# Turning x by VectorE instead of ScalarE, transform results by ScalarE alone, and a new order of all engines, in a spectral and state-space mix

## The chip, the cores and the metric

The kernel runs on one core of one Trainium2 chip. The metric is the device time of one execution in microseconds (us); lower is better. Each engine (TensorE for matmuls, VectorE, ScalarE, GpSimd, and SyncE, which only issues DMAs) works through its own list of instructions in the order in which the program gives them, and waits at an instruction until what it needs is there.

## The reference

One input x of 2048 rows (time) and 1024 columns goes two ways, and a gate per row mixes the results:

```python
x = A_x                                                    # (1, 2048, 1024), bf16
g = _sigmoid((x * gate_w).sum(-1, keepdims=True))
a = irfft2(rfft2(x) * (w_r + 1j * w_i))                    # over both axes
# the state-space way, for each t in turn:
h = Lam_bar[None, :] * h + Bu[:, t, :]                     # Bu = x @ B_bar.T, complex, 1024 states
b = 2.0 * (hseq @ Cmat.T).real + x * Dskip
return g * a + (1 - g) * b
```

## The kernel before

**Turning x.** Both ways need x with its columns on the partitions. The rows are taken in 16 groups: group j holds the 128 rows `16 p + j`. Groups 0 to 11 are loaded as they are into tiles `xn` (L242, called `CT` in the trace, because the space is used again for C later), turned by TensorE into a PSUM tile `pt` (L919, 8 transposes of 128 by 128 per group), and copied from there into the big tile `xQ` by ScalarE (L929). Groups 12 to 15 come turned from a transposing DMA (L238) and are copied into `xQ` by ScalarE from SBUF (L925). In `xQ` time stands as chunk c (8 chunks of 256), half g (2), group j (16), step q (8); the p of a group is thus `(c, q, g)`, and the copy L929 reads `pt` with a step of two elements, so that the halves g come apart. The trace gives every such copy as 128x1024, bf16.

**The spectral way, at the beginning.** `fold()` (L943 to L954, VectorE) makes sums and differences of columns out of `xQ` for each group or pair of groups into `preT`, TensorE multiplies by a cosine table (`fd`, L433 to L443), the result goes to SBUF as `X` (`fd_out`, L449, 16 casts of 128x1024 from PSUM), TensorE does the first stage along time (`s1`, L462), and the result goes to SBUF as `CT`, `A` or `A_last` (`s1_out`, L474, 16 casts of 128x1024 from PSUM). Of these casts VectorE does 4 of L449 (`FD_DVE`) and 3 of L474 (`S1_DVE`), ScalarE the rest. For some groups a mirror matmul (L970) and two sums of VectorE (L976, L977) come between. From there the results go through DRAM to later stages.

**The state-space way.** For each of the 8 chunks `unit_mm` (L398) multiplies all of `xQ` of that chunk with `BT`, in four units of 32 matmuls; it cannot begin before all 16 groups are in `xQ`. ScalarE casts each unit to `h` (L408). VectorE then does the recurrence of the chunk on `h`: products with tables `tab` (L347, L350), sums (L353, L356), two scans (L363), products again, and sums (L374, L378). The tables `tab` are made once at the beginning by `make_tab`, four times over: VectorE makes an angle (L281, L1106, L1108), ScalarE its sine and cosine and their products `t` (L1110, L1111, L1113, L292, L298), VectorE the last two tables (L302, L307). The result `h` is multiplied with C by TensorE (L713, and L727 for the last three tiles of 128 rows). The very last operations are L727 for the last chunk, the closing sum on VectorE (L899), and a store. L892 (VectorE) prepares what L899 adds; L825 to L846 (VectorE) make the output of the spectral way out of its last matmuls.

**The order.** It is written out by hand: the string `ORDER` has one letter for each step of each function above (`T` a transposed group, `U` its copy, `f` a step of `fold`, `F` and `E` `fd` and its cast, `S` and `A` `s1` and its cast, `t` a step of `make_tab`, `h` and `H` a unit of `unit_mm` and its cast, `v` the next step of the recurrence, which `PIECES` then names), and each engine gets its instructions in the order in which the letters stand. `SLOTS` names for each PSUM tile in turn which of four places it takes. SyncE issues nearly all DMAs in that same order. `FILL_V`, `FILL_T` and `WARM` set matmuls without use ahead of the first ones, and are the same in both kernels.

Of the kernel before, what the change touches and what calls it, by code (L numbers as in the profile page):

```python
# [26 lines left out]
NCH = S // TC  # L27
# [5 lines left out]
NTURN = 12  # L33
# [4 lines left out]
FD_DVE = (2, 4, 6, 7)  # L38
# [3 lines left out]
S1_DVE = (1, 4, 5)  # L42
CLOSES = (0, 1, 2, 3, 10, 4, 5, 11, 12, 6, 7, 8, 9)
PIECES = (
# [6 lines left out]
)  # L51
SLOTS = (
    "0123012310231023102310230123012031201312031203101230132031231031201312303312013213021021013010320130",
    "1220123203201320130130120321023120320321021023120312301230231201302303120",
# [3 lines left out]
    "xxxTVUVVVaTfVVrrUGTGG|Tfaaa|UafFffftafftUftxFEfTETUFffU22xSEkSTSTArxAfffUAUFTTEUfffUFbxwxbxbbTUEFbfE",  # L58
    "1bT~SSUfuFSFAUUUU2bbtbfAF1AtbbtrFttrbEffE11EbEh11SStbttfttttAg1~HtfufhA~tetFSSFrKHrtu1EAvfAEhtttvttt",
    "SSFtbbvvvAtEttH1Avthtftv1cttwv1tcthccctttvtcch~HFtvftHvvhuHtvfStEettStAHhtAeKrvFctcvvFhEEHKtvwtcSvtS",  # L60
    "hvvKc1vcc1vAAKKvv1c1v1hcvswcsLMvvveHHekMYsssnNHvvhHnsvvvJWWMvs3vsvNvvsssssnvssnvvs4NMvv4Njvhv553vhvv",
    "YvyJJL46H4vv5WWvhh5vvvMM78Jj7HHmn3nHvv8M44m6MnN77WW5jv+Yy5vvv3M845+mNY8nMJJMyvvv+467hvHMh5vN7N34vHmh",
    "4J8m+6n3h8v77HmH+55v4n64JMvNnMYy5vW83n+v7N474vJ568vYmmNJ7dh7NWj+v58v5vyvvd88MhvHHm8+MJm6h+n378vv7Hh8",
    "J+d4Y4YX5vv5NnJH6XXv7ny7mNNm8+hn8hvqivvvvvJvqyHihYivvyiqhivqqiYvNImvni+qJJmHIIiini+HinvdIIH+vvIIIqIN",
    "IiiiNmI+vvIInvvImvyJqii%NJINIJYJYmhvvv+vvvlylzvhHmplpzZZH+mZZZhlZvhPPRR++zyRRRlQDQHzRZZmRHZ+ZRZvoOZD",
    "QvlpDzzPovOvQBvZZlpPYvZZvBZDZRDRRRvzQDoloOBzoQOopZOoPOBlzlZRoDDZZvBZZRpQvzCvYZZvZZBZZPRDoQoo9RQQ9yRR",
    "0RRyCooD099C9Y990DD0D0Y00",
# [75 lines left out]
def kernel(  # L143
# [82 lines left out]
    x_v = x.rearrange("(p j) d -> p j d", j=16)  # L226
# [7 lines left out]
    def load_x():  # L234
        for i in range(8):
            if i >= NTURN // 2:
                g = i - NTURN // 2
                nc.sync.dma_start_transpose(out=xt[:, :, :, g].rearrange("p j d s -> p (j d) s"), in_=x_sg[g][:, NTURN * D:])  # L238
                yield
                continue  # L240
            for js in (slice(0, 1), slice(1, 2)) if i == 0 else (slice(0, 2),):
                nc.sync.dma_start(out=xn[i][:, js], in_=x_v[:, 2 * i + js.start:2 * i + js.stop, :])  # L242
                yield
# [678 lines left out]
    def turn_out():  # L922
        for j in range(16):
            if j >= NTURN:
                nc.scalar.copy(out=x_gjq[:, :, :, :, j, :].rearrange("p c d g q -> p d g c q"),  # L925
                               in_=xt[:, j - NTURN].rearrange("p d g (c q) -> p d g c q", c=NCH))
                yield
                continue
            nc.scalar.copy(out=x_gjq[:, :, :, :, j, :].rearrange("p c d g q -> p d c g q"),  # L929
                           in_=pts.pop(j).rearrange("p d (c q g) -> p d c g q", c=NCH, g=2))  # L930
# [285 lines left out]
```

## Time and profile before

| | before |
|---|---|
| time, median of 3 runs (lowest to highest) | 305.25 us (305.02 to 307.25) |
| profiled execution: span from first to last instruction | 303.6 us |
| TensorE busy | 296.4 us (98%) |
| VectorE busy | 289.3 us (95%) |
| ScalarE busy | 188.5 us (62%) |
| GpSimd busy | 73.3 us (24%) |
| HBM traffic | 166 GB/s over the span |

The profiled execution is recorded by its span alone, 303.6 us. The median of the runs lies 1.65 us above it, the lowest run 1.42 us; that part stands before the first or after the last instruction, or is the difference between one execution and another. TensorE's granted clock is full throughout (0.999). Busy time of TensorE is modelled on pipelined matmuls and includes short gaps between dependent ones, so its 98% doesn't mean that all of it is work. Durations of neighbouring VectorE instructions overlap a little, so that the sum of single durations is larger than the busy time.

### The profile page before, as it was taken

What the parts mean: (1) busy time and instruction counts of PE and PEld (TensorE: products, weight loads), DVE (VectorE), ACT (ScalarE), POOL (GpSimd) and SP (SyncE); (2) the same over time, 40 slices, a digit from 0 to 9 for tenths busy, and PEclk for the clock granted to TensorE, in tenths of its full rate; (3) what the DMA queues carried; (4) which work ended last, traced back from release to release, by engine and by line L of the source; (5) the groups of instructions that cost most, each with busy time, mean ns of one, the idle gap of its engine ahead of it and who ended that gap; (6) DMA issues with size and microseconds to landing.
All of it is one profiled execution on the core that took longest, in us unless ns stands there. A gap on an engine that the chain in (4) does not pass through costs nothing. (4 is left out here: it accounts for less than half of the span.)

```text
span 303.6 us, 6402 instructions
## 1 busy us (share of the span) xinstructions
PE 296.4 (98%) x2568; PEld 197.4 (65%) x2592; DVE 289.3 (95%) x340; ACT 188.5 (62%) x255; POOL 73.3 (24%) x99
## 2 busy tenths in 40 slices
PE   8999999999999999999999999999999999999995
PEld 5664677878864685458553866669657986645543
DVE  2999999999999999999999999999899999999995
ACT  4999999896532383667665865529668774343400
POOL 2100420745893001110210220202011253252330
PEclk9999999999999999999999999999999999999999
DMA  6999999989999599895948798687758876978976
GB/s 208 341 201 194 253 193 310 162 142 154 268 214 241 160 259 219 181 250 189 212 96 258 163 223 225 139 294 147 242 174 185 165 88 135 160 132 143 165 153 181
DMA packets 74157, 59.35 MB, mean 196 GB/s; under 512 B 44904, under 2 KB 61680, under 8 KB 74128
## 3 DMA queue, kind: packets, MB, share of 16 engines
q1 hardware_dynamic: 66560, 49.82, 65.8%
q0 software_dynamic: 6912, 8.69, 23.0%
q10 hardware_dynamic: 656, 0.44, 0.5%
q8 instruction: 20, 0.33, 0.4%
q14 instruction: 9, 0.07, 0.1%
HBM read 27.46 MB, written 23.08 MB: 166 GB/s over the span
## 5 line engine op out<-in xcount | busy, mean ns | idle before, releaser
L398 PE MATMUL psu<-xQ,BT 128*128 128x256 bf16 x1024 | 116.5, 273 | 0.2 <-DVE X L449 0.2
L398 PEld LDWEIGHTS <-BT 128*128 128x128 bf16 x1024 | 99.0, 98 | 17.3 <-issue 4.6
L713 PE MATMUL ps_y<-CT,h 128*128 128x512 bf16 x397 | 92.5, 379 | 0.9
L363 DVE TENSOR_TENSOR_SCAN h<-rz,h 128x2048 bf16<-128x2048 f32 (+1 forms) x20 | 70.8, 3561 | 0.0
L713 PEld LDWEIGHTS <-h 128*128 128x128 bf16 x416 | 39.6, 98 | 46.3 <-issue 2.9
L785 POOL DMA_DIRECT2D y_scratch<-su x20 | 17.3, 902 | 135.7 <-ACT su L779 105.4
L408 ACT CAST h<-psu 128x1024 bf16<-128x1024 f32 x32 | 32.3, 1011 | 18.7 <-PE psu L398 13.1
L350 DVE TENSOR_TENSOR h<-h,tab 128x4096 bf16<-128x4096 bf16 (+1 forms) x20 | 37.1, 1859 | 0.1
L744 ACT ACTIVATE ye<-ps_y,omg 128x512 f32<-128x512 f32 x26 | 17.9, 689 | 26.3 <-PE ps_y L713 11.8
L347 DVE TENSOR_TENSOR xQ<-h,tab 128x4096 bf16<-128x4096 bf16 x12 | 27.4, 2284 | 1.0 <-ACT h L408 1.0
L603 ACT CAST X<-ps_s 128x1024 bf16<-128x1024 f32 x16 | 16.2, 1010 | 14.6 <-PE ps_s L594 11.2
L727 PE MATMUL ps_q<-CT,h 128*128 128x512 bf16 (+2 forms) x110 | 21.3, 348 | 0.2
L817 ACT ACTIVATE BT<-ps_id,gB 128x1024 bf16<-128x1024 f32 x14 | 15.3, 1114 | 9.9 <-PE ps_id L810 5.7
L671 ACT CAST ZT<-ps_is 128x1024 bf16<-128x1024 f32 x16 | 15.8, 1017 | 6.2 <-PE ps_is L661 6.2
L637 ACT CAST C<-ps_is 128x1024 bf16<-128x1024 f32 x16 | 15.7, 1011 | 5.1 <-DMA xQ<-in_A_x_dram 3.4
L851 POOL DMA_DIRECT2D BT<-y_scratch x10 | 13.1, 1452 | 19.7 <-DVE BT L846 13.3
L727 PEld LDWEIGHTS <-h 128*128 128x128 bf16 x112 | 10.3, 98 | 10.4 <-DVE h L378 0.5
L779 ACT ACTIVATE su<-xs,omg 128x512 f32<-128x512 bf16 x20 | 14.2, 723 | 4.1 <-DMA y_scratch<-su 2.2
L929 ACT COPY xQ<-pt 128x1024 bf16<-128x1024 bf16 x12 | 12.2, 1082 | 1.3 <-PE pt L919 1.3
L449 ACT CAST X<-ps_fd 128x1024 bf16<-128x1024 f32 x12 | 12.3, 1062 | 1.0 <-PE ps_fd L439 0.9
L617 DVE TENSOR_TENSOR UV<-X,Wb 128x2048 bf16<-128x2048 bf16 x8 | 9.6, 1220 | 0.6 <-ACT ye L744 0.6
L617 DVE TENSOR_TENSOR UV<-X,raw 128x2048 bf16<-128x2048 bf16 x8 | 9.8, 1223 | 0.2 <-ACT X L604 0.2
(200 smaller groups left out, 397.3 us busy)
## 6 DMA issues: line engine op xcount, KB each, us to landing
y_scratch<-ye SPq DMA_DIRECT2D x20, 256.0 KB, 4.6
y_scratch<-su POOLq DMA_DIRECT2D x20, 256.0 KB, 4.7
Bb<-turn_scratch SPq DMA_DIRECT2D x16, 256.0 KB, 5.2
turn_scratch<-C SPq DMA_DIRECT2D x16, 256.0 KB, 4.1
raw<-turn_scratch SPq DMA_DIRECT2D x8, 512.0 KB, 4.3
xs<-in_A_x_dram SPq DMA_DIRECT2D x13, 256.0 KB, 3.9
out_dram<-BT SPq DMA_DIRECT2D x11, 256.0 KB, 4.3
CT<-in_A_x_dram SPq DMA_DIRECT2D x5, 512.0 KB, 6.1
```

Source lines behind the costliest of these rows:

```text
L347: nc.vector.tensor_mul(out=tmps["s"], in0=u[:, ::-1], in1=bc(i))
L350: nc.vector.tensor_mul(out=u, in0=u, in1=bc(i))
L363: nc.vector.tensor_tensor_scan(out=seg, data0=rz[:, js.start + j:js.start + j + m].rearrange("p j t -> p (j t)"), data1=seg, initial=0.0, ...
L398: nc.tensor.matmul(psu[:, j, :], lhsT=BT[4 * q + j][:, ri, d8, :], rhs=xQ[:, c, d8, :], start=(d8 == 0), stop=(d8 == 7))
L408: nc.scalar.copy(out=hs[c][:, ri, 4 * q:4 * q + 4].rearrange("p b (q j) -> p b q j", j=32), in_=psus.pop((c, q, ri)).rearrange("p b (j q) ...
L603: nc.scalar.copy(out=X2, in_=ps2s[g][b])
L617: nc.vector.tensor_mul(out=UV, in0=X2s.pop((g, b)).unsqueeze(1).to_broadcast([P, 2, 2, K]), in1=fft["Wb"][g // 2 % 2][:, :, at:at + 1, :]. ...
L671: nc.scalar.copy(out=ZT[:, 4 * kp:4 * kp + 4, :, 4 * G:4 * G + 4].rearrange("p (c r) n g -> p c r n g", c=2), in_=pszs.pop((G, kp)).rearra ...
L713: nc.tensor.matmul(psy, lhsT=hs[c][:, ri, jb, P * tq:P * (tq + 1)], rhs=CT[ri][:, jb, 512 * dh:512 * (dh + 1)], start=(i == 0), stop=(i == ...
L727: nc.tensor.matmul(psq, lhsT=hs[c][:, ri, jb, P * tq:P * (tq + 1)], rhs=CT[ri][:, jb, at:at + n], start=(i == 0), stop=(i == 15))
L744: nc.scalar.activation(out=ye, in_=psys[tb][:, K * hf:K * (hf + 1)], func=ACT.Copy, scale=omg[:, tb:tb + 1])
L785: nc.gpsimd.dma_start(out=y_dram[tb, hf], in_=xgs[tb, hf], accum_op=ALU.add)
```

## The change

Four things are changed together.

1. x is loaded with `(g, s)` on the partitions instead of `(s, g)`: the two halves of a group stand apart, 64 partitions each. The bytes and the pieces of the DMA are the same. The transposed `pt` then has the order `(g, c, q)`, and the copy into `xQ` reads it from one end to the other, without a step.
2. All 16 copies of turned x (12 from PSUM, 4 from SBUF; one line, L928, in the changed kernel) go to VectorE (`TURN_DVE`), from ScalarE.
3. The 7 casts of transform results that VectorE did (4 of L449, 3 of L474) go to ScalarE (`FD_DVE` and `S1_DVE` are empty).
4. `ORDER`, `PIECES` and `SLOTS` are written anew.

Lines behind L928 have a number that is lower by one in the changed kernel.

```diff
-FD_DVE = (2, 4, 6, 7)
+FD_DVE = ()
...
-S1_DVE = (1, 4, 5)
+S1_DVE = ()
+TURN_DVE = tuple(range(16))
...
 ORDER = (
-    "xxxTVUVVVaTfVVrrUGTGG|Tfaaa|UafFffftafftUftxFEfTETUFffU22xSEkSTSTArxAfffUAUFTTEUfffUFbxwxbxbbTUEFbfE",
...
+    "xTxxGGGUffTxV|VfVVU2VVaaf|TFTfUkffFxabxfT2UTxftf2ESFEAfUUfxTTxFrrTSbbfrfEESSUUfUAAAbtftftTUbFEFwbbbb",
...
-    x_v = x.rearrange("(p j) d -> p j d", j=16)
+    x_v = x.rearrange("(s g j) d -> g s j d", g=2, j=16)
...
-                nc.sync.dma_start(out=xn[i][:, js], in_=x_v[:, 2 * i + js.start:2 * i + js.stop, :])
+                nc.sync.dma_start(out=xn[i][:, js], in_=x_v[:, :, 2 * i + js.start:2 * i + js.stop, :])
...
     def turn_out():
         for j in range(16):
-            if j >= NTURN:
-                nc.scalar.copy(out=x_gjq[:, :, :, :, j, :].rearrange("p c d g q -> p d g c q"),
-                               in_=xt[:, j - NTURN].rearrange("p d g (c q) -> p d g c q", c=NCH))
-                yield
-                continue
-            nc.scalar.copy(out=x_gjq[:, :, :, :, j, :].rearrange("p c d g q -> p d c g q"),
-                           in_=pts.pop(j).rearrange("p d (c q g) -> p d c g q", c=NCH, g=2))
+            if j < NTURN:
+                src = pts.pop(j).rearrange("p d (g c q) -> p d g c q", g=2, c=NCH)
+            else:
+                src = xt[:, j - NTURN].rearrange("p d g (c q) -> p d g c q", c=NCH)
+            (nc.vector.tensor_copy if j in TURN_DVE else nc.scalar.copy)(
+                out=x_gjq[:, :, :, :, j, :].rearrange("p c d g q -> p d g c q"), in_=src)
             yield
```

What the new order does on the engines that the prediction speaks of is shown at three places. Each row has the line, the operation, and what it writes and reads; in brackets stands whom it waits for.

The first place is the start of VectorE's list, behind its two memsets. Before:

```order
L1082 CAST vecF<-vps 128x24 [waits PE_49]
L1084 CAST tau_f<-tau_i 128x256 [waits Pool_49]
L943 TENSOR_TENSOR preT<-xQ 128x512 [waits Activation_49]
L1088 TENSOR_TENSOR are<-dt,vecF 128x8 [waits Activation_49]
L1089 SCALAR_TENSOR_TENSOR ang_154<-dt,vecF 128x8
L945 TENSOR_TENSOR sums<-xQ 128x512
```

In the changed kernel:

```order
L928 COPY xQ<-pt 128x16x8x8 [waits PE_49]
L942 TENSOR_TENSOR preT<-xQ 128x512 [waits DVE_49]
L944 TENSOR_TENSOR sums<-xQ 128x512
L1081 CAST vecF<-vps 128x24 [waits PE_49]
L947 TENSOR_TENSOR preT<-sums 128x256 [waits DVE_49]
L949 TENSOR_TENSOR preT<-sums 128x256
```

VectorE begins with the copy of the first turned group and folds it at once; the copy of the turned vectors (`vecF`), with which it began before, comes fourth.

The second place is ScalarE's list around the first products `t` of `make_tab` (L292), where the turned x ended before. Before:

```order
L474 CAST CT_82<-ps_s_505 128x1024 [waits PE_49]
L925 COPY xQ<-CT_83 128x16x8x8 [waits DMAHW5_49,DMAHW3_49]
L925 COPY xQ<-CT_83 128x16x8x8 x3
L1110 ACTIVATE rot_kk<-ang 128x512 [waits DVE_49]
L1111 ACTIVATE sn_f<-ang 128x512
L1113 ACTIVATE cs_f<-rot_kk,chpi 128x512 [waits Activation_49]
L292 ACTIVATE t_584<-sn_f,ci 128x256 [waits Activation_49]
```

In the changed kernel:

```order
L474 CAST CT_82<-ps_s_552 128x1024 [waits PE_49]
L449 CAST X_575<-ps_fd 128x1024 [waits PE_49,Activation_49]
L1112 ACTIVATE cs_f<-rot_kk,chpi 128x512
L449 CAST X_593<-ps_fd 128x1024 [waits PE_49,Activation_49]
L408 CAST h<-psu 128x1024 [waits PE_49]
L474 CAST A_128<-ps_s_654 128x1024 [waits PE_49]
L292 ACTIVATE t_665<-sn_f,ci 128x256 [waits DVE_49]
```

The four copies of the turned x are gone from here, and the first L292 now stands behind the cast of the first unit of `unit_mm` (L408) and behind one more cast of the first stage (L474), while the sine and cosine were made earlier.

The third place is VectorE's list around its last sums of the last chunk, L374 and L378. Before:

```order
L350 TENSOR_TENSOR h<-h,tab 128x4096 [waits DVE_49]
L892 SCALAR_TENSOR_TENSOR xQ<-xs,omg,BT 128x1024 [waits DVE_49]
L374 TENSOR_TENSOR h<-h,xQ 128x2048 [waits DVE_49]
L825 TENSOR_TENSOR BT<-BT 128x2x2x128 [waits DMASW6_49,DMASW0_49,Activation_49]
L827 TENSOR_TENSOR BT<-BT 128x2x2x128
L378 TENSOR_TENSOR h<-h,xQ 128x2048
```

In the changed kernel:

```order
L350 TENSOR_TENSOR h<-h,tab 128x4096 [waits DVE_49]
L374 TENSOR_TENSOR h<-h,xQ 128x2048 [waits DVE_49]
L825 TENSOR_TENSOR BT<-BT 128x2x2x128 [waits DMASW7_49,DMASW6_49,Activation_49]
L378 TENSOR_TENSOR h<-h,xQ 128x2048
L827 TENSOR_TENSOR BT<-BT 128x2x2x128
L836 TENSOR_TENSOR BT<-BT 128x4x256 [waits DVE_49]
L838 TENSOR_TENSOR BT<-BT 128x4x256
L892 SCALAR_TENSOR_TENSOR xQ<-xs,omg,BT 128x1024
```

One L892 and one L827 have moved from ahead of the last sum L378 to behind it.

More of the change, by code (lines that the diff above doesn't have):

```diff
@@ L41 @@
 CARRY_POOL = ()
[L42 removed]
+S1_DVE = ()
+TURN_DVE = tuple(range(16))
 CLOSES = (0, 1, 2, 3, 10, 4, 5, 11, 12, 6, 7, 8, 9)
 PIECES = (
[6 rows of a table removed]
[5 rows of a table added]
 )
 SLOTS = (
[L53 to L54 removed]
+    "0123013201320132013201320132013201320130213203120313201032130230120310210101230123012302132131203120",
+    "3102310210310231023021210320312031031203201321302130230123010132012301230",
 )
```

18 lines of the change are left out of this document (9 added, 9 removed), and 11 rows, old and new, of the table PIECES.

## Prediction

> **What bounds the kernel now.** I began with the slices of the span, to see which engines are full and where.
>
> ```profile
> DVE  2999999999999999999999999999899999999995
> ACT  4999999896532383667665865529668774343400
> ```
>
> VectorE (DVE) is full from the second slice to the last but one; ScalarE (ACT) only in the first eight, about 60 us. TensorE's row is full too, but its busy time is modelled. So I asked next for the busy time in six stretches: until VectorE begins, until the first big matmul (L398), to 60 us, to the end of VectorE's last sum of the last chunk, to the last L899, and the rest.
>
> ```profile
> core 0: us, PE busy (x) PEld busy (x) DVE busy (x) ACT busy (x) POOL busy (x), PEclk, DMA share, GB/s
> 0.00:6.06 6.06, 4.85 (x24) 2.51 (x25) 0.33 (x2) 2.08 (x2) 0.98 (x7) 1.00 0.66 207
> 6.06:30.20 24.14, 22.68 (x214) 14.98 (x217) 23.25 (x60) 23.66 (x33) 2.56 (x12) 1.00 1.11 243
> 30.20:60.00 29.80, 29.67 (x276) 22.86 (x277) 28.86 (x48) 27.27 (x43) 11.38 (x20) 1.00 1.16 230
> 60.00:286.56 226.56, 225.43 (x1980) 149.95 (x1998) 223.21 (x212) 134.62 (x180) 55.91 (x58) 1.00 0.86 187
> 286.56:300.81 14.25, 13.76 (x78) 7.07 (x79) 13.70 (x21) 0.86 (x1) 2.42 (x2) 1.00 0.86 201
> 300.81:303.60 2.79, 0.00 (x0) 0.00 (x0) 0.00 (x0) 0.00 (x0) 0.00 (x0) 0.93 0.19 57
> ```
>
> VectorE's idle time is 5.73 us at the start (6.06 less 0.33), then 0.89, 0.94, 3.35 and 0.55, and 2.79 behind its last instruction, in which the last store lands. Between start and end that makes 5.73 in 294.75 us. The chain of work that ended last says who holds the end:
>
> ```profile
> 285.42 1.15 DVE h L378
> 286.61 5.79 PE ps_q L727 x26
> 292.44 7.99 PE ps_q L727 x52
> 300.46 0.35 DVE raw L899
> ```
>
> TensorE's last 13.8 us wait for VectorE's last sum L378; ahead of it the chain is VectorE throughout, back to 269 us. VectorE's list, with its few waits, is thus the bound, and TensorE follows it closely.
>
> ```profile
> DVE vecF L1082 <- PE vps L1080: 4.9, 1, 4.9
> DVE preT L943 <- ACT xQ L929: 0.2, 1, 0.2
> DVE preT L943 <- PE pt L919: 0.2, 1, 0.2
> ```
>
> In the beginning VectorE waits little for ScalarE's copies: 0.2 us, and 0.2 for the transposes before them.
>
> **The change, part by part.** The start first.
>
> ```profile
> 4.17 1.06 PE L919 MATMUL pt<-ident,CT 128*128 128x128 bf16 x8
> 5.27 1.01 ACT L929 COPY xQ<-pt 128x1024 bf16<-128x1024 bf16 x1 [1.28 <-PE pt L919]
> 6.06 0.18 DVE L1082 CAST vecF<-vps 128x24 f32<-128x24 bf16 x1 [4.91 <-PE vps L1080]
> ```
>
> The first turned group is ready at 5.27. VectorE now begins with its copy, then 0.79 us earlier than with `vecF`. The load of x moves the same pieces, and its first DMAs keep their places in SyncE's queue, so I cost it at nothing; nothing hides it at this place, and each us that the first group came later would be one of the end. **Start: -0.79.**
>
> The copies and casts. No row shows a VectorE copy of bf16 from PSUM without a step, so these are the nearest ones:
>
> ```profile
> L449 DVE CAST X<-ps_fd 128x1024 bf16<-128x1024 f32 x4 | 4.9, 1216 | 0.0
> L474 DVE CAST CT<-ps_s 128x1024 bf16<-128x1024 f32 x3 | 3.6, 1216 | 0.0
> L945 DVE TENSOR_TENSOR sums<-xQ 128x1024 bf16<-128x1024 bf16 x6 | 4.5, 755 | 0.0
> L1106 DVE TENSOR_SCALAR rot_kk<-ang 128x512 f32<-128x512 f32 x4 | 1.7, 418 | 0.0
> L547 DVE COPY Bcol<-aps 32x128 bf16<-32x128 bf16 x1 | 0.3, 272 | 0.0
> ...
> 28.97 1.22 DVE L449 CAST X<-ps_fd 128x1024 bf16<-128x1024 f32 x1
> 30.10 0.68 DVE L943 TENSOR_TENSOR preT<-xQ 128x1024 bf16<-128x1024 bf16 x1
> 30.70 1.11 DVE L945 TENSOR_TENSOR sums<-xQ 128x1024 bf16<-128x1024 bf16 x1
> ```
>
> Neighbours overlap: from start to start a cast takes 1.13 us (28.97 to 30.10) and a bf16 operation on 1024 elements in the same short runs of `xQ` 0.60 (30.10 to 30.70), 0.08 under its duration. A copy from PSUM lies between these two, 0.60 and 1.13. I take 0.60: the copy, like L943, has bf16 on both sides and unit steps, while L449 reads f32. L547, bf16 from PSUM, speaks for the slow end (272 ns for 128 elements), but reads with a step. For a copy from SBUF, L1106 moves the same 2048 bytes from one source in 0.42, so 0.34 from start to start; the other end is 0.60, and I take 0.34, as it has one source. Added: 12 x 0.60 + 4 x 0.34 = 8.56. Removed: 7 x 1.13 = 7.91. **Copies: +0.65**, with +1.7 if the SBUF copies cost 0.60, and +7.0 if the PSUM copies cost 1.13.
>
> The Trainium skill ("VectorE: DVE Perf Modes", "The perf-mode tier table") caps a copy with a PSUM operand at two elements a cycle and gives an SBUF copy of bf16 four; by it the sum would be what it is. No row of this trace shows it. The same page ("Rules for kernel authors") tells elsewhere to accept one element a cycle on a PSUM source; by that the sum would be the slow one, and it is a rival below.
>
> ScalarE loses 16 copies and gains 7 casts; does this bring the first L398 forward? It needs the last copy into `xQ`.
>
> ```profile
> 25.51 4.03 ACT L925 COPY xQ<-CT 128x1024 bf16<-128x1024 bf16 x4
> 30.33 3.65 PE L398 MATMUL psu<-xQ,BT 128*128 128x256 bf16 x32 [0.19 <-DVE X L449]
> 10.21 0.17 DVE L1135 TENSOR_TENSOR lb<-SC,r_sb 128x16 f32<-128x16 f32 x1
> 10.92 0.16 DVE L1143 TENSOR_TENSOR ci<-num 128x8 f32<-128x8 f32 x1
> ```
>
> Before, it ended at 29.54 on ScalarE. Now it stands on VectorE behind the same folds and angles as L943 at 30.10 did, with 16 copies (8.56) in place of 6 casts (6.78) and ten small operations (eight run from 10.21 to 11.08, so 1.1 in all), which come later now. That is +0.7, less 0.79 for the start: it ends at 30.0. VectorE takes ScalarE's place as what the beginning waits for, and the big matmuls begin at about 30.1 and not much earlier than at 30.33.
>
> ```profile
> 33.91 1.04 PE L462 MATMUL ps_s<-X,raw 64*128 64x512 bf16 x8
> 33.85 0.41 DVE L948 TENSOR_TENSOR preT<-sums 128x512 bf16<-128x512 bf16 x1
> 35.17 0.88 DVE L307 SCALAR_TENSOR_TENSOR tab<-sn_f,cr,t 128x256 bf16<-128x256 f32 x2
> 24.78 0.69 DVE L977 TENSOR_TENSOR preT<-preT,ps_r 128x512 bf16<-128x512 bf16 x1
> 30.96 1.03 ACT L292 ACTIVATE t<-sn_f,ci 128x256 f32<-128x256 f32 x2
> 35.47 1.02 ACT L408 CAST h<-psu 128x1024 bf16<-128x1024 f32 x1
> ```
>
> TensorE has done more by then: two groups more of L462, 1.04 us. But the mirror matmul behind the first unit needs an L943 that stands on VectorE 4.4 us behind the last copy (two operations of 0.60, the small ones 1.1, four of `fold` 1.32 as from 33.85 to 35.17, and 0.68): 34.4, while the unit ends at 30.1 + 3.65 = 33.75. So it gives back 0.65 and is some 0.6 ahead, which the end doesn't show as long as VectorE holds it.
>
> The wait that the order adds: the first `t` stands behind the cast of the first unit (L408) and that of a group whose L462 follow the mirror. Mirror at 34.4, L462 and latencies to 35.4, cast to 36.4, half of L292 to 36.9. VectorE comes to L302, which needs it, after L945 and two of 0.69: 34.4 + 0.60 + 1.4 = 36.4. **New wait: +0.5**; everything of VectorE is queued behind L302. The waits of 0.2 each on L929 and `pt` have the work between them laid anew; I let them go: **-0.4**. The 3.35 + 0.94 us of idle time from 30 to 286 I leave as they are, for want of a reason that the profile shows.
>
> The end.
>
> ```profile
> L892 DVE SCALAR_TENSOR_TENSOR xQ<-xs,omg,BT 128x1024 f32<-128x1024 bf16 x3 | 3.8, 1277 | 0.0
> L827 DVE TENSOR_TENSOR BT<-BT 128x512 bf16<-128x512 bf16 x7 | 2.9, 419 | 0.0
> 300.46 0.35 DVE L899 SCALAR_TENSOR_TENSOR raw<-ps_q,omg,xQ 128x128 bf16<-128x128 f32 x1 [0.28 <-PE ps_q L727]
> ```
>
> An L892 (1.28) and an L827 (0.34 from start to start) go behind the last sum. That brings L378 forward by 1.62, but what VectorE has to do behind it grows from 13.70 to 15.3, over TensorE's 13.8. VectorE then sets the end, without the idle 0.55 that it has there now: **-0.55**, and the moving itself gives nothing.
>
> Sum: -0.79 + 0.65 + 0.5 - 0.4 - 0.55 = -0.59 on the span of 303.6, and so 303.0. The runs' median stands 1.65 above the profiled span, and I keep that: 304.7.
>
> **The rivals.** *The new order closes gaps* (faster). Of VectorE's 4.29 idle us between 30 and 286, three go, since every engine's list is new and ScalarE is no longer full there: 304.7 - 3.0 = 301.7. For it: on a list this full each us of a wait is a us of the end. Against it: TensorE would have to gain them too, and it idles only 1.26 us in those two stretches; what it could gain is density in the first 30 us, where it ran 214 matmuls in 24 us, and that hangs on copies that now end no earlier.
>
> *The table loop* (slower). L292 behind L408 makes a ring: VectorE's L943, the mirror on TensorE, the cast on ScalarE, `t`, and VectorE's L302. I gave it 0.5 us. There are four tables, and each stands between such casts; at 1.1 us more for each the ring costs 4.4, which gives 309.1. It decides from 3.6 us of added waits on. For it: VectorE has nothing else to do at an L302. Against it: ScalarE has nine copies less to do in the beginning on balance, about 1.0 us each as in the row of L929, and so comes sooner to whatever has been made ready.
>
> *One element a cycle from PSUM* (slower). 12 x 0.53 more, 6.4 us: 311.1. For it speak L547 and the page's second rule; against it that L943 reads and writes such runs at two a cycle. The Trainium skill ("Vector Engine (DVE) Microarchitecture Reference", "5.1 Performance modes") asks for unit steps and 2-byte types on all operands for two a cycle, and puts no bar on PSUM; that is what the new load provides.
>
> *Nothing moves*: ScalarE's relief is off the path, as costed; that is within the forecast.
>
> **How the numbers follow.** The forecast 0.60, its own range 303.0 to 306.5 (SBUF copies at 0.60 add 1.0, the uncosted 0.4 of waits and the ring half a us each way); gaps closed 0.20, around 301.7; the ring 0.13, around 309.1; one a cycle 0.07, around 311.1. About 1% (3 us) is what a measurement of this kernel can tell from no change. The range from 301.0 to 309.0 holds the forecast, most of the faster case and half of the ring. Faster by over 1% (under 302.2): 0.20, with the lower tail of the forecast 0.22. Slower (over 308.3): 0.17. Within: 0.61.
>
> **What would show it.** L928 from PSUM near 0.68 us and from SBUF near 0.42 (1.22 would be the slow rival). VectorE's first copy near 5.3 us, the last one near 30, the first L398 within half a us of 30.3. A wait of VectorE for L292 or L298 of about 0.5, not several. No idle time between L378 and the last L899. I am wrong if VectorE's idle time between 30 and 286 changes by more than 2 us, if TensorE turns out to hold the end with its last L727 well after VectorE is ready, or if the first transposes start late.

## The result and the profile after

| | before | changed |
|---|---|---|
| time, median of four runs (lowest to highest) | 305.77 us (305.02 to 307.25) | 360.21 us (358.35 to 365.14) |
| ratio, 95% interval | | 1.1765 (1.1712 to 1.1818) |
| span of the profiled execution | 303.6 us | 356.5 us |
| VectorE busy | 289.3 us | 293.2 us |
| TensorE busy | 296.4 us | 309.9 us |
| ScalarE busy | 188.5 us | 180.1 us |
| first L398, last L398 begin | 30.3, 250.4 us | 80.1, 300.7 us |

The change makes the kernel 18% slower, far outside the range of 301 to 309. One of the changed kernel's four runs, 365.14 us, was a slow one, and the ratio leaves it out. The slices of the span tell where the time goes. Of the page of the changed kernel, VectorE's busy tenths, the granted clock of TensorE and the share of the DMA engines in 40 slices of 8.9 us:

```profile
DVE  0233321569999999999999999999999999899995
...
PEclk9976565889999999999999999999999999999998
DMA  1411939199998999987998898636899914999697
```

VectorE is no longer full from the second slice but from the tenth. TensorE's clock falls to 0.5 in slices five and seven, while it waits for x between its transposes, where it had been full throughout. The DMA engines, at four tenths or more in every slice before, show ones in slices one, three, four and eight. The same six stretches as in the prediction, cut at the first copy of VectorE, the first L398, 30 us behind it, the end of VectorE's last sum L378, and the end of its last L899:

```profile
core 0: us, PE busy (x) PEld busy (x) DVE busy (x) ACT busy (x) POOL busy (x), PEclk, DMA share, GB/s
0.00:10.15 10.15, 4.20 (x15) 1.66 (x15) 0.33 (x2) 1.28 (x1) 0.98 (x7) 1.00 0.10 35
10.15:80.10 69.95, 36.39 (x232) 21.89 (x233) 25.60 (x61) 18.89 (x26) 2.81 (x14) 0.73 0.75 93
80.10:110.00 29.90, 28.69 (x270) 22.42 (x268) 28.75 (x57) 25.27 (x41) 14.27 (x21) 1.00 0.99 182
110.00:337.87 227.87, 226.84 (x2001) 150.09 (x1998) 223.79 (x209) 134.68 (x181) 48.08 (x55) 1.00 0.85 192
337.87:352.68 14.81, 13.81 (x79) 7.07 (x79) 14.78 (x23) 0.00 (x0) 2.45 (x2) 1.00 0.97 179
352.68:356.50 3.82, 0.00 (x0) 0.00 (x0) 0.00 (x1) 0.00 (x0) 0.00 (x0) 0.68 0.52 172
```

VectorE's idle time is 9.82 us ahead of its first copy (5.73 before) and 44.35 us from there to the first L398 (0.89 before). These two make 47.55 of the 52.9 us; from the first L398 on the kernel takes 276.4 us against 273.3. VectorE's waits say for what. The columns are the line, whom it waited for, us in all, times, the longest:

```profile
DVE xQ L928 <- PE pt L919: 44.4, 9, 9.7
...
PEld L919 <- DMA CT<-in_A_x_dram: 42.5, 7, 8.3
PE pt L919 <- DMA CT<-in_A_x_dram: 38.3, 7, 7.4
```

VectorE waits for the transposes, and the transposes wait for the load of x. What SyncE issued first, in the kernel before and then in the changed one (start and length on SyncE's queue):

```profile
0.73 1.34 SPq L242 DMA_DIRECT2D CT<-in_A_x_dram  x3
2.12 2.06 SPq L252 DMA_DIRECT2D G_sb<-c_G  x3
```

```profile
0.72 5.01 SPq L242 DMA_DIRECT2D CT<-in_A_x_dram  x3
5.78 7.57 SPq L252 DMA_DIRECT2D G_sb<-c_G  x3
15.00 0.53 SPq L242 DMA_DIRECT2D CT<-in_A_x_dram  x1
```

The same three loads of x take 5.01 us on the queue instead of 1.34, and everything behind them comes later. From 4 to 9 us, with little but x under way, the DMA engines move 49 GB/s at a share of 0.13, as much as 2 of 16 engines that are busy all the time, where the kernel before moves 304 GB/s at 0.90. Before and changed (VectorE's busy time, the clock, the share and GB/s):

```profile
4.00:9.00 5.00, 2.83 (x14) 1.00 0.90 304
```

```profile
4.00:9.00 5.00, 0.00 (x0) 1.00 0.13 49
```

```profile
9.08 1.04 PE L919 MATMUL pt<-ident,CT 128*128 128x128 bf16 x8 [4.70 <-DMA CT<-in_A_x_dram]
```

The first transposes begin at 9.08 us instead of 4.17, the last ones at 76.3 instead of 22.5.

The prices of the copies, on the other hand, are those forecast. The groups by line of the changed kernel (busy us, mean ns, idle before):

```profile
L928 DVE COPY xQ<-pt 128x1024 bf16<-128x1024 bf16 x12 | 8.3, 689 | 44.5 <-PE pt L919 44.4
L928 DVE COPY xQ<-CT 128x1024 bf16<-128x1024 bf16 x4 | 1.4, 416 | 0.0
```

And the end belongs to VectorE, as forecast. The chain that ended last holds no TensorE any more; its last pieces of any length are:

```profile
347.53 2.40 DVE xQ L892 x2
...
350.50 1.40 DVE raw L899 x2
...
352.42 0.26 DVE raw L899
```

### The profile page after: what moved, and what is told of

It is laid out like the page before. It is cut to its first block, busy times and chain, and to the rows that moved or that the text cites. A ratio compares the mean times of both kernels' runs of the same rounds, so it can differ in the third digit from the quotient of the medians.

```text
span 356.5 us, 6429 instructions
## 1 busy us (share of the span) xinstructions
PE 309.9 (87%) x2592; PEld 203.1 (57%) x2592; DVE 293.2 (82%) x349; ACT 180.1 (51%) x246; POOL 68.6 (19%) x99
## 5 line engine op out<-in xcount | busy, mean ns | idle before, releaser
L398 PE MATMUL psu<-xQ,BT 128*128 128x256 bf16 x1024 | 116.2, 273 | 1.2 <-DMA BT<-in_B_B_re_dram 1.1
L398 PEld LDWEIGHTS <-BT 128*128 128x128 bf16 x1024 | 99.0, 98 | 18.3 <-issue 4.6
L363 DVE TENSOR_TENSOR_SCAN h<-rz,h 128x2048 bf16<-128x2048 f32 (+1 forms) x20 | 71.1, 3577 | 0.1
L928 DVE COPY xQ<-pt 128x1024 bf16<-128x1024 bf16 x12 | 8.3, 689 | 44.5 <-PE pt L919 44.4
L919 PE MATMUL pt<-ident,CT 128*128 128x128 bf16 x96 | 11.4, 298 | 38.3 <-DMA CT<-in_A_x_dram 38.3
L785 POOL DMA_DIRECT2D y_scratch<-su x20 | 18.5, 950 | 131.5 <-ACT su L779 105.5
L408 ACT CAST h<-psu 128x1024 bf16<-128x1024 f32 x32 | 32.1, 1012 | 14.2 <-PE psu L398 14.2
L919 PEld LDWEIGHTS <-CT 128*128 128x128 bf16 x96 | 9.1, 137 | 44.3 <-DMA CT<-in_A_x_dram 42.5
L744 ACT ACTIVATE ye<-ps_y,omg 128x512 f32<-128x512 f32 x26 | 17.0, 687 | 30.4 <-PE ps_y L713 20.1
L449 ACT CAST X<-ps_fd 128x1024 bf16<-128x1024 f32 x16 | 16.3, 1017 | 27.5 <-PE ps_fd L443 26.0
L817 ACT ACTIVATE BT<-ps_id,gB 128x1024 bf16<-128x1024 f32 x14 | 14.9, 1114 | 12.8 <-DMA out_dram<-BT 11.0
L474 ACT CAST CT<-ps_s 128x1024 bf16<-128x1024 f32 x8 | 7.6, 1028 | 16.6 <-PE ps_s L462 16.6
```

Source lines behind the costliest of these rows:

```text
L363: nc.vector.tensor_tensor_scan(out=seg, data0=rz[:, js.start + j:js.start + j + m].rearrange("p j t -> p (j t)"), data1=seg, initial=0.0, ...
L398: nc.tensor.matmul(psu[:, j, :], lhsT=BT[4 * q + j][:, ri, d8, :], rhs=xQ[:, c, d8, :], start=(d8 == 0), stop=(d8 == 7))
L408: nc.scalar.copy(out=hs[c][:, ri, 4 * q:4 * q + 4].rearrange("p b (q j) -> p b q j", j=32), in_=psus.pop((c, q, ri)).rearrange("p b (j q) ...
L449: (nc.vector.tensor_copy if j in FD_DVE else nc.scalar.copy)(out=X1.rearrange("p r (m e c) -> p r m e c", e=2, c=2), in_=psf.pop(j).rearra ...
L744: nc.scalar.activation(out=ye, in_=psys[tb][:, K * hf:K * (hf + 1)], func=ACT.Copy, scale=omg[:, tb:tb + 1])
L785: nc.gpsimd.dma_start(out=y_dram[tb, hf], in_=xgs[tb, hf], accum_op=ALU.add)
```

## The experiments

Two questions: is it the load, and what is it about the load; and does the rest of the change, with the load mended, do what the prediction said.

### The load alone, and the change without its cause

The new load put alone into the kernel before (ScalarE's copies read the columns in their new order):

```diff
-    x_v = x.rearrange("(p j) d -> p j d", j=16)
+    x_v = x.rearrange("(s g j) d -> g s j d", g=2, j=16)
```

> The kernel before with the new load alone: x comes with its halves apart, ScalarE still copies (it reads the turned x without a step). If the load is the cause (each DMA of x, its source walked half by half, runs on 2 of the 16 DMA engines, at the 52 GB/s seen in the changed kernel), the 3.1 MB of x take some 60 us instead of 17, and the time is 350 to 365 us, with a DMA share near 0.13 in stretches where only x comes. If the new order or VectorE's copies are the cause, it is 305 us.

Measured: 356.42 us in a single run, span 354.6. The load alone brings all but some 4 us of the loss.

The change with each load of x cut into its two halves:

```diff
-                nc.sync.dma_start(out=xn[i][:, js], in_=x_v[:, :, 2 * i + js.start:2 * i + js.stop, :])
+                for g in range(2):
+                    nc.sync.dma_start(out=xn[i][64 * g:64 * (g + 1), js], in_=x_v[g, :, 2 * i + js.start:2 * i + js.stop, :])
```

> The changed kernel, with each DMA of x cut in two, one for each half of 64 partitions: the same bytes from the same addresses to the same places. If the number of DMA engines is the cause, each of them walks 64 pieces outermost, runs on all 16, and the time is what was forecast for the rest of the change, 301 to 309 us. If the addresses (rows of a half lie 64 KB apart, not 32) or the order of the engines are the cause, it stays at 350 to 360 us.

Measured: 315.25 us (313.74 to 315.78), ratio 1.0322 (1.0295 to 1.035). The same bytes from the same addresses to the same partitions, in twice as many DMAs, save 45 us, so these 45 are not of the distance between the rows, nor of the order. The time stays above the 301 to 309 expected, however.

The change with the load as before; VectorE's copies then read `pt` in steps of two:

```diff
-    x_v = x.rearrange("(s g j) d -> g s j d", g=2, j=16)
+    x_v = x.rearrange("(p j) d -> p j d", j=16)
...
-                src = pts.pop(j).rearrange("p d (g c q) -> p d g c q", g=2, c=NCH)
+                src = pts.pop(j).rearrange("p d (c q g) -> p d g c q", c=NCH, g=2)
```

> The changed kernel with the old load (rows of a group in order) and VectorE's copies reading the turned x with a step of two. If the load is the cause it is quick again; the 12 copies from PSUM then cost about 1.22 us each if the step matters to VectorE (307 to 314 us), or 0.69 as in the changed kernel if not (302 to 307 us). If the order is the cause: 355 us.

Measured: 315.25 us (314.26 to 316.76), ratio 1.0327 (1.0288 to 1.0367), a little above the 307 to 314 expected if the step matters. The groups by line show what the step costs VectorE:

```profile
L928 DVE COPY xQ<-pt 128x1024 bf16<-128x1024 bf16 x12 | 14.5, 1219 | 4.5 <-PE pt L919 4.5
```

1219 ns against 689 with unit steps. So the copies did need what the new load was to provide, at 12 x 0.53 = 6.4 us.

### How many parts

The kernel before, with its rows loaded in four parts of 32, and in eight of 16:

```diff
-    x_v = x.rearrange("(p j) d -> p j d", j=16)
+    x_v = x.rearrange("(s g j) d -> g s j d", g=4, j=16)
```

> The kernel before with each group's 128 rows loaded in four parts of 32 (one DMA, the parts outermost), with nothing else changed, so that x's rows stand permuted and the output is another one, from the same work. If a DMA runs on as many engines as it has parts, the load runs at twice the 52 GB/s, about 100, the 3.1 MB take some 30 us, and the time is 318 to 330 us. If the distance of the rows is the cause (now 128 KB), it is as slow as two parts or slower, 355 us and more.

> The kernel before, its x load with 8 parts of 16 rows instead of one range of 128 (rows come permuted, so that the output is another). With 2 parts x came at 49 to 52 GB/s and the kernel took 356 us, with 4 parts 330 us. Theory that a load is spread over as many DMA engines as it has parts: 8 parts bring some 200 GB/s, and the time is 305 to 313 us, a DMA share near 0.5 while only x is loaded. Rival, that the loss is one of split loads in general and not proportional to the parts: 325 us or more.

Measured: 330.46 and 317.5 us, a single run each, the second above the 305 to 313 expected. Stretches from 3 to 4 us, where little but x is loaded, in the kernel before with two parts (the load alone, above), four and eight (the last two columns are the share of the DMA engines and GB/s):

```profile
3.00:4.00 1.00, 1.00 (x4) 0.19 (x2) 0.00 (x0) 0.75 (x1) 0.00 (x0) 1.00 0.12 33
```

```profile
3.00:4.00 1.00, 1.00 (x4) 0.19 (x2) 0.00 (x0) 0.53 (x1) 0.00 (x0) 1.00 0.30 66
```

```profile
3.00:4.00 1.00, 1.00 (x4) 0.19 (x2) 0.00 (x0) 1.00 (x1) 0.00 (x0) 1.00 0.39 152
```

The first transposes begin at 9.24, 7.15 and 5.08 us. The loss is not of split loads as such: it shrinks with each doubling of the outermost dimension, from 51 to 25 to 12 us (each against some 305). Shares of 0.12, 0.30 and 0.39 in single microseconds go up with the parts but don't tell 4 and 8 engines exactly (0.25 and 0.5).

The traces also record every packet of a DMA, and so how many are under way at one moment. Counted are the packets of 2048 bytes (a row of x is as long) on the queue of these loads, from 2.5 to 3.0 us: mostly 16 in the kernel before, two at every moment with two parts, four at every moment with four. With eight parts it is two to seven at first, and eight in the median from 3.5 to 4.5 us. A packet takes 84 ns, in the median of the first 200, in each of these runs. So the parts set how many packets go at once, and not how long one takes.

The Trainium skill ("DMA: Bandwidth & Descriptors", "Why a DMA increments its semaphore by 16 and not by 1") says that a DMA is spread over the largest number of engines, at most 16, that divides the outermost dimension larger than one of both its sides. By it the old load (128 partitions outermost on both sides) has 16 engines and the new one (2 halves outermost at the source) has 2: the trace agrees, with 16 and two packets at a time, and a share of 0.13 against 2/16.

### What two DMAs cost by themselves

The kernel before with the new load as two DMAs for each; the same with the new assignment of the copies, in the old order; and the change with the second half of each load issued from ScalarE's queue:

```diff
+                for g in range(2):
+                    nc.sync.dma_start(out=xn[i][64 * g:64 * (g + 1), js], in_=x_v[g, :, 2 * i + js.start:2 * i + js.stop, :])
...
+                    (nc.sync, nc.scalar)[g].dma_start(out=xn[i][64 * g:64 * (g + 1), js], in_=x_v[g, :, 2 * i + js.start:2 * i + js.stop, :])
```

> The kernel before, with the new load made as two DMAs for each of its old ones (one for each half of 64 partitions) and ScalarE's copies reading the columns in their new order; order and engines as before. Theory that two DMAs of 64 partitions are as good as one of 128 with the old pattern: 304 to 307 us, and so the other 10 us of the 315 measured with two DMAs and everything else of the change are of the order or of the engines. Rival, that two DMAs at the head of SyncE's queue bring the first groups later and make up those 10 us: 312 to 316 us.

> Load as two DMAs and all turn copies on VectorE, the seven copies of the beginning on ScalarE, as in the change, but the order of the steps, the pieces and the PSUM slots of the kernel before. Theory that the new order costs the 10 us that stay once the load is mended: 304 to 308 us. Rival, that VectorE's 16 copies cost them whatever the order (more VectorE work ahead of the first scan, a longer chain through the first groups): 312 to 318 us.

> The change with each x DMA cut into its two halves of 64 partitions, the second half issued by ScalarE's queue instead of SyncE's. Both on SyncE's queue it took 315.25 us, where the queue spent 3.85 us on the first six x DMAs instead of 1.34 on three, so that what stands behind came 4 to 5 us later. Theory that this delay of SyncE's queue is the price of two DMAs: 309 to 312 us, nearer to the kernel with the old load. Rival, that DMAs of 64 partitions are slower on their way whatever queue issues them: 314 to 316 us.

Measured: 311.04 (1.0192, 1.0163 to 1.0221), 311.29 (1.0202, 1.0169 to 1.0235) and 315.44 us (1.0323, 1.0248 to 1.0399). The first two lie just under the ranges of their rivals, the third in its rival's. Two DMAs in place of one cost 5.7 us by themselves; behind that later load the copies on VectorE cost nothing more (so the second rival has its time, but not by its mechanism), and the new order the other 4 us (315.25 against 311.29). SyncE's queue with two DMAs for each load:

```profile
0.72 3.85 SPq L243 DMA_DIRECT2D CT<-in_A_x_dram  x6
4.61 1.53 SPq L253 DMA_DIRECT2D G_sb<-c_G  x3
```

Six issues take 3.85 us where three took 1.34, and the cosine table behind them is issued at 4.61 instead of 2.12. But to halve the issues on SyncE's queue brought nothing: on two queues the first copy of VectorE even comes at 7.83 us instead of 5.09, since ScalarE issues the second halves only from 2.93 us on, behind five small loads. Two DMAs do have more packets under way than one DMA with the halves outermost (8 and 13 in the median, from 2.5 to 3.0 and from 3.0 to 3.5 us, in the first of these runs), but not steadily 16. What a load of two halves costs beyond the issue isn't settled.

### The change with its load mended

The halves can be set apart without touching the load. TensorE turns x by multiplying with an identity; a permuted identity puts the columns of `pt` where they are wanted:

```diff
+    apart = cpool.tile([P, P], BF16, name="apart")
+    nc.vector.tensor_copy(out=apart.rearrange("p (g s) -> p g s", g=2), in_=ident.rearrange("p (s g) -> p g s", g=2))
...
-                nc.tensor.transpose(out=pt[:, i, :], in_=xn[j // 2][:, j % 2, P * i:P * (i + 1)], identity=ident)
+                nc.tensor.transpose(out=pt[:, i, :], in_=xn[j // 2][:, j % 2, P * i:P * (i + 1)], identity=apart)
```

With this (called the mended change from here on) the change keeps everything but its load. The second run has the old order with it.

> The change with the load of x as before (one DMA for 128 rows), the halves being set apart by TensorE: the turns multiply by a permuted identity, which VectorE makes once from the identity (128x128, in the idle time ahead of the first rows of x). VectorE's 12 copies from PSUM read in steps of one, so that nothing of the change is left out but its load. Theory that all the loss over 305 us was the load's (few engines, or the longer issue of two DMAs): 303 to 306 us, as the prediction had it. Rival, that the new order of the steps costs some 4 us of its own (315.25 against 311.29 with two DMAs): 308 to 310 us.

> The same (old load, permuted identity, VectorE's 16 turn copies, ScalarE's seven transform copies), but with the order of steps, pieces and PSUM slots of the kernel before. Theory that the other engines for the copies cost nothing by themselves (311.29 against 311.04 with two DMAs) and only the load did: 304 to 306 us. If VectorE's copies cost something that the late load had hidden: 307 us or more.

Measured: 310.41 (308.24 to 310.67; ratio 1.0149, 1.0104 to 1.0194) and 308.64 us (308.52 to 308.88; ratio 1.0109, 1.0075 to 1.0144). So the load is not all: with it mended 5.3 us stay. In the old order the new copies hold up the beginning (first L398 at 33.8 us instead of 30.3); the new order mends that (30.6), and is lost elsewhere. The six stretches of the first of these runs (it has two lines more, so L398 is L400 here):

```profile
core 0: us, PE busy (x) PEld busy (x) DVE busy (x) ACT busy (x) POOL busy (x), PEclk, DMA share, GB/s
0.00:5.57 5.57, 3.68 (x19) 1.75 (x20) 0.51 (x4) 1.28 (x1) 0.98 (x7) 1.00 0.66 203
5.57:30.60 25.03, 24.19 (x233) 15.67 (x231) 24.76 (x61) 18.61 (x26) 2.84 (x14) 1.00 1.11 240
30.60:60.00 29.40, 29.36 (x278) 23.20 (x277) 28.95 (x58) 26.03 (x41) 16.65 (x25) 1.00 1.02 196
60.00:290.16 230.16, 227.45 (x1993) 150.26 (x1992) 223.32 (x208) 133.84 (x180) 45.05 (x52) 0.99 0.84 188
290.16:304.98 14.82, 13.86 (x80) 7.07 (x79) 14.78 (x23) 0.00 (x0) 2.45 (x2) 1.00 0.91 177
304.98:308.90 3.92, 0.00 (x0) 0.00 (x0) 0.00 (x0) 0.00 (x0) 0.00 (x0) 0.98 0.50 167
```

VectorE's idle time is 5.06, 0.27, 0.45, 6.84, 0.04 and 3.92 us, where it was 5.73, 0.89, 0.94, 3.35, 0.55 and 2.79. Its busy time is 292.3 instead of 289.3. So of the 5.3 us that the span is longer, 3.0 are busy time, 3.5 idle time between 60 us and the last sum L378, and 1.1 the last store, while the start, the stretch to 60 us and the end give back 0.7, 1.1 and 0.5. The idle time that was added lies in one wait; from the list of waits:

```profile
DVE BT L827 <- ACT BT L819: 5.2, 1, 5.2
```

It ends at 264.8 us. VectorE's spectral sum L827 (L825 before) waits for ScalarE's copy L819 (L817 before), and that waits 4.83 us for a store of the output to free the tile that it writes:

```profile
263.67 2.12 ACT L819 ACTIVATE BT<-ps_id,gB 128x1024 bf16<-128x1024 f32 x2 [4.83 <-DMA out_dram<-BT]
```

That store, the second of the two in the first row below, was issued at 255.6 us and landed 7.7 us later; the median of these stores is 3.3. Right behind it SyncE issued two transposes of x, which the new order puts between the stores:

```profile
252.46 3.45 SPq L861 DMA_DIRECT2D out_dram<-BT  x2
255.96 6.13 SPq L1160 DMA_TRANSPOSE xQ<-in_A_x_dram  x2
262.26 1.51 SPq L861 DMA_DIRECT2D out_dram<-BT  x2
```

### The one wait

Three theories were tried on it. First, the two transposes (`X` in the string) moved back beside the first one, and, in the second run, the permuted identity made by GpSimd; in the third the kernel before with its two transposes moved late:

```diff
-    "mvnN+3v4Y4v5hvm+nN+vJvymnY56Nnd87vh887vv8hmYyJNqiivJhvHHvqqIqXii+v+IHHvmmYini+viiIqnJIviiIIvIvynI+vv",
+    "mvnN+3v4Y4v5hvm+nN+vJvymnY56Nnd87vh887vv8hmYyJNqiivJhvHHvqqIqXXXii+v+IHHvmmYini+viiIqnJIviiIIvIvynI+",
...
-    "RvPPOozzPXvvX+ZZZZQQvRllRloZORBRDm+oZvBDvzzZZRZZlOovRQDDoZZOzQvvBBDzOZDvZZZYooCYBYOYRZRZQ99RRBDyRDRQ",
+    "PlRvPPOozzPvv+ZZZZQQvRllRloZORBRDm+oZvBDvzzZZRZZlOovRQDDoZZOzQvvBBDzOZDvZZZYooCYBYOYRZRZQ99RRBDyRDRQ",
```

> The change with the load as before and the permuted identity (310.41 us), but two of SyncE's three transposes of x into tiles of xQ (made beside the last tiles' products) go back from between the stores of the output to right behind the first one, which is some 60 us earlier, as the kernel before has them. Theory that these two transposes hold the stores back on the DMA queue, so that ScalarE's spectral copies wait for a tile, and behind them VectorE (5.2 us in one piece near 260): 305 to 306 us, and that one wait under 1 us. Rival, that VectorE's wait there comes of the new order of ScalarE's and VectorE's steps themselves: still 309 to 311 us, the wait 4 us or more.

> The same as the run with the transposes early, and the permuted identity made by GpSimd instead of VectorE, where it had stood ahead of the A memset, waited 1.3 us for the identity and let TensorE's warming start at 1.9 us instead of 1.2. Theory that the first VectorE copy's start (5.57 us instead of 5.09) goes one to one into the end: 0.4 to 0.6 us less than that run, 304 to 305.5 us, within 0.5% of the kernel before. Rival, that the start is hidden: no difference.

> The kernel before with nothing changed but those two transposes of x, put from behind the first one (at 186 to 189 us of its profile) to behind the third late sum, between the stores of the output. Theory that they hold the stores and so ScalarE and VectorE: 308 to 311 us, VectorE waiting 3 to 5 us in one piece between 255 and 270. Rival, that they only matter together with the new order of the other engines: 304 to 306 us.

Measured: 310.06 (307.96 to 311.25; ratio 1.0127, 1.0077 to 1.0176), 309.18 (307.97 to 310.7; 1.0107, 1.0069 to 1.0145) and 305.31 us (304.93 to 309.08; 1.0005, 0.9973 to 1.0038). The wait in the first run:

```profile
DVE BT L827 <- ACT BT L819: 3.7, 2, 2.2
```

It shrinks from 5.2 to 3.7 in two, the time does not change by what the runs can tell, and the kernel before doesn't mind late transposes at all: a copy of ScalarE waits there 5.4 us for a store, instead of 3.3, but VectorE waits no longer for such a copy than it did (0.4 us). As an account of the time the theory falls. The 0.9 us between the first two runs agree with a start that counts one to one (first copy at 4.96 us instead of 5.95), but their ranges overlap.

Second, VectorE's order: in the new one the last chunk's two scans (L363) stand behind the sums that wait, in the old one a scan stands ahead of a pair of them, and the theory was that it covers the wait:

```profile
261.74 4.42 DVE L363 TENSOR_TENSOR_SCAN h<-rz,h 128x2048 bf16<-128x2048 f32 x1
```

One scan put ahead (two letters `v`, for the carry and the scan), both put ahead, and the reverse in the kernel before:

```diff
-    "PlRvPPOozzPvv+ZZZZQQvRllRloZORBRDm+oZvBDvzzZZRZZlOovRQDDoZZOzQvvBBDzOZDvZZZYooCYBYOYRZRZQ99RRBDyRDRQ",
+    "PlRvPPOozzPvvvv+ZZZZQQRllRloZORBRDm+oZBDvzzZZRZZlOovRQDDoZZOzQvvBBDzOZDvZZZYooCYBYOYRZRZQ99RRBDyRDRQ",
```

> As the run with the transposes early and GpSimd's permuted identity (309.18 us), but in VectorE's order the last chunk's carry and the first of its two scans (0.22 and 4.42 us) stand ahead of the spectral sums for whose input VectorE waited 3.1 us, and not behind them. Theory that the new order put the last scans behind sums that wait for ScalarE, which waits for a store of the output to free its tile, while the scans were ready: the wait vanishes behind the scan, 305.5 to 306.5 us. Rival, that VectorE's wait there is no part of the path (the end is set by the stores or by TensorE): 308.5 to 309.5 us.

> The same with both scans of the last chunk ahead of those sums. Theory as above: the wait is gone, 305 to 307 us, no better than with one scan, since one (4.4 us) covers 3.1 us. If the sums, their tiles and the stores then come late in their turn and set the end: 308 us or more.

> The kernel before with one step of VectorE's order moved: the first of the last chunk's two scans, which stood ahead of a pair of spectral sums at 262 us, goes behind them, beside the second scan, as the change has it. ScalarE's copy for those sums waited 3.29 us there for a store and ended at 266.9, so VectorE would have to wait from about 262.9 to 267. Theory: 308 to 310 us and one wait of some 4 us. Rival, that the kernel before has slack there: 304.5 to 306 us.

Measured: 308.93 (307.36 to 310.65; ratio 1.0118, 1.0086 to 1.0149), 312.54 (311.79 to 313.35; 1.0226, 1.0203 to 1.0248) and 305.12 us (304.63 to 306.37; 0.9996, 0.9983 to 1.001). The first run's waits:

```profile
DVE raw L901 <- DMA out_dram<-raw: 3.5, 1, 3.5
...
DVE BT L827 <- ACT BT L819: 0.8, 1, 0.8
```

The wait near 260 is gone as meant (the 0.8 us are at 243), and VectorE waits 3.5 us at its last sums instead, for a tile that a late store still holds. Both scans ahead make it worse (the wait near 260 is gone there too, but one of 3.2 us near 288 and one of 3.3 at the last sums come in its place, as the second half of its expectation has it). The kernel before loses nothing by the new place of the scan, but this run did not do what its expectation says. Its trace has the pair of sums that went ahead of the scan, and the copy of ScalarE that waits for a store:

```profile
262.65 0.42 DVE L825 TENSOR_TENSOR BT<-BT 128x512 bf16<-128x512 bf16 x1
265.04 1.11 ACT L817 ACTIVATE BT<-ps_id,gB 128x1024 bf16<-128x1024 f32 x1 [2.93 <-DMA out_dram<-BT]
```

The pair begins at 262.65 without a wait, ahead of the end of that copy, which thus belongs to later sums. In the kernel before, the copy ahead of that one ended at 262.5, soon after the scan began at 261.74, so there too the scan had hardly anything to cover. So the reverse is no test of the theory, and it is the first two runs that speak against it: right on the wait alone, it does not account for the time.

Third, the end as a whole. From the first spectral sum on (near 241 us) the steps are put into the order of the kernel before, behind the start of the mended change; and the other way round:

```diff
-    "vvNqqNqvviiinivvJyvm+hiiIIIvvmvvIhJvv%N+NIIvIIlYyHHzlppzmZhZZlPlZZhPzzZpQRRQHRppRovJHRRpJZZZlZDRZZvD",
+    "vvNqqNqvviiinivvJyvm+hiiIIIvvmvvIhJvv%N+NIIvIIlYyHHzlppzmJJlZZZZZhlZhPPRR+zRRRlQDQHzRZZmRHZ+ZRZvoOZD",
...
```

(`PIECES` and `SLOTS` are changed to fit, in both runs.)

> The mended change (old load, permuted identity by GpSimd, transposes early: 309.18 us) with its own order up to the first spectral sum of the end (near 241 us), and the order of the kernel before for all steps from there on. Theory that the beginning of the change gains some 0.5 to 1 us (the last product L398 of the recurrence starts at 249.4 us against 250.4 before) and its end loses 3 to 5 us: 304 to 305.5 us. Rival, that what the mended change lacks against the kernel before is lost ahead of that point: 308 to 310 us.

> The kernel before with its own order up to the first spectral sum of the end, and the order of the mended change for all steps from there on. Theory that the new order of the end alone costs its 3 to 5 us: 308 to 310 us. Rival, that the end's order costs nothing behind the old start: 304.5 to 306 us.

Measured: 308.4 (307.59 to 310.63; ratio 1.0101, 1.0066 to 1.0136) and 308.28 us (307.69 to 310.96; 1.011, 1.007 to 1.015). VectorE's wait in the one and in the other (the lines are L825 and L817, shifted):

```profile
DVE BT L818 <- ACT BT L810: 4.4, 2, 4.0
```

```profile
DVE BT L815 <- ACT BT L807: 3.7, 1, 3.7
```

The new end costs 3 us behind the old start as well, by a wait at the same place near 260. But the old end behind the new start costs as much, by a wait of 4.0 near 250 that neither kernel has: ScalarE reaches L810 late, behind a cast that waits 3.37 us for TensorE. So each half of the new order (the first with VectorE's copies) costs some 3 us where the other half is the old one, and both together cost hardly more (309.18 against 308.4 and 308.28). It isn't shown that the new start is free of blame. What sets the length of the wait near 260 stays open too: the profile puts the wait of ScalarE's copy down to a store in two of the runs (4.83 us in the mended change, 2.15 with the transposes early) and to TensorE in two others (3.14 us with GpSimd's identity, 3.90 with the new end behind the old start). No version tried beats the kernel before.

## Why the prediction was wrong

- **The load, costed at nothing: the step that failed.** "The load of x moves the same pieces, and its first DMAs keep their places in SyncE's queue, so I cost it at nothing." Both halves of the sentence are true and say nothing of how many pieces go at a time, which fell from 16 to two. The load runs at 49 GB/s from 4 to 9 us instead of 304, alone it takes the kernel from 305 to 356 us, and VectorE waits 44.4 us for the transposes behind it. The next words, that nothing hides it and each us that the first group came later would be one of the end, held for the whole of x: the first L398 is 49.8 us late and the span 52.9 longer. "If the first transposes start late" was among the signs of being wrong, and it is the one that came.
- **The start, -0.79.** With the load mended VectorE's first copy begins at 5.57 us (with the permuted identity made by VectorE) and 4.96 (by GpSimd), and in the first case the idle time ahead of it is 0.67 us shorter: right as far as the runs can tell (a third run, with VectorE's identity, has 5.95), under the condition that the load left it.
- **The copies, +0.65.** The prices were right, 689 and 416 ns by the rows against 0.68 and 0.42 forecast, so that the rival of one element a cycle is refuted by the row (1219 ns, with a step of two, is near that rival's price). The Trainium skill ("VectorE: DVE Perf Modes", "The perf-mode tier table") allows two elements a cycle with a PSUM operand, and the trace agrees: 1024 elements take 0.53 us less with unit steps. VectorE's busy time grew by 3.0 us in the mended run, however, not by 0.65. 0.3 are the permuted identity, and 1.2 lie in two lines whose work the change doesn't touch: the six calls of L948 on 512 elements take 542 ns each instead of 419, and L1135 586 instead of 165. Why they do is not known, and the other 0.8 were not traced to a line.
- **The first L398 near 30.1, the last copy at 30.0.** 30.6 and 29.7 in the mended run: right.
- **The new wait at L302, +0.5.** No wait of VectorE at L302 is in the list of the mended or the changed kernel; too high by 0.5, and the rival of the table loop is refuted with it, as far as these two go (in the old order, with the copies on VectorE, there is one of 0.5 at L307).
- **The small waits, -0.4, and the gaps that close.** From the first copy to 60 us VectorE idles 0.72 us instead of 1.83: more gained than forecast.
- **"The 3.35 + 0.94 us of idle time from 30 to 286 I leave as they are, for want of a reason that the profile shows": the second step that failed.** In the mended run the first of them is 6.84 us, by one wait of 5.2 near 260, in which VectorE waits for a copy of ScalarE and that for a store. The new order of the end was not followed through to it. In the changed kernel itself the two make 5.23 us instead of 4.29, so that there it hardly shows behind the load. With this wait, the busy time above and the last store below, the forecast fails even with the load mended, 310.4 against 304.7.
- **The end, -0.55.** VectorE sets it, with 0.03 us of idle time between L378 and its last instruction in the changed kernel, where there were 0.55: right. The last store then lands 1.1 us later behind VectorE's last instruction than before (3.92 against 2.79 in the mended run), which the sum did not have.
- **The rivals.** None of the four was this mechanism. The range could not hold it, because the term behind it had been given no bounds at all.

## What to carry to other kernels

Before a rearranged DMA is costed at nothing, look at the outermost dimension of its two sides: with two, four and eight steps there, this load had two, four and eight packets under way at a time, though partitions and bytes stayed the same. A row order that a matmul with a permuted identity can make needs no other load. And where an order is written by hand for one kernel, a new order asks to be followed to the end: here each half of the new one, put together with the other half of the old, cost some 3 us, though single steps could be moved in the old one at no cost.

## What the runs showed of the hardware that was not expected

- A slow load blocks the queue that issues it: three loads with two packets under way at a time held SyncE for 5.01 us instead of 1.34, and the next table's three for 7.57 instead of 2.06.
- TensorE's granted clock falls when TensorE idles: 0.73 on average from 10 to 80 us in the changed kernel, down to 0.5 in single slices, while it was full throughout before; the transposes took 298 ns in the mean, against 229 before. It was full again from the stretch of the first L398 on. In the mended run it fell once more in the wait near 260: TensorE is busy 1.37 of 4.00 us from 262 to 266, and the clock is 0.80 in this stretch and 0.77 in the next 4 us.
- Two DMAs of 64 partitions in place of one of 128 cost 5.7 us at the head of this kernel, on one queue, and no less on two.
- A transpose by a permuted identity costs no more than by the identity (220 ns in the mean against 229 before), and needs one copy of 128x128 (0.34 us on VectorE) ahead of it.
